# Row pairs of a query projection in two groups a step, with other places for four kinds of copies

## The chip, the cores and the metric

The kernel runs on one NeuronCore of a Trainium2 chip. The metric is the device time of one execution in microseconds (us), as a median over runs. Beside these runs there is one profiled execution, from which the profile page and the trace come; its own time is given with its span, which is the time from its first to its last instruction.

## The reference

Two kinds of layer, A and B, each used twice with the same weights, on x of 2048 tokens with 448 features:

```
x = x + A(layernorm(x));  x = x + B(layernorm(x))
x = x + A(layernorm(x));  x = x + B(layernorm(x))

A: mem = mem0 (8 rows)
   for each segment s of 32 tokens (64 segments):
       h = concat(mem, x[s])                  # 40 rows
       q, k, v = h Wq, h Wk, h Wv             # 16 heads of 256
       o = softmax(mask(q k^T / 16)) v Wo     # masked: mem rows see all, others are causal
       mem = o[:8];  out[s] = o[8:]
B: h = relu(x W_gate) * (x W_up);  out = h W_down      # 1792 hidden
```

The memory rows of a segment come out of the segment before, so layer A is a recurrence of 64 steps, run twice.

## The kernel before

Before the loop the kernel folds Wq and Wk of each head into one 448 x 448 matrix (`A_sb`, `A3`, `A3z`) and Wv and Wo into another (`B_sb`). The main loop runs over steps `g` from 0 to 68 (`step`, L610). In a step the first layer A works on segment g (chain 0) and the second layer A on segment g - 4 (chain 1), side by side in the columns of the same matmuls. Steps 0 to 3 and 64 to 67 have one chain, steps 4 to 63 have two. Every second step also carries layer B for blocks of tokens (`Feed`, L419): here it is called a feed step, the others plain steps.

The query projection of a step multiplies 448 features. 384 of them are done in wide matmuls of 128 rows, three for each of 56 tiles of weights (`close_bank`, L532). The last 64 features need only 64 rows, so two such matmuls with different row halves of TensorE run as a row pair (`open_banks`, L519). Ten PSUM banks are filled: for half 0 of the heads banks 0 to 3 (six tiles each, called b0 to b3 in the code) and a tail bank z0 (four tiles); for half 1 c0 to c3 and z1. Before the change a bank is opened by its row pairs and closed by its wide matmuls. The order at the start of a step is: pairs of b0, b2; close both; pairs of b1, b3, z0, z1; close z0, b1, b3, z1; transposes of the layer's input (`kps`, in `hk_make`) and pairs of c0 to c3; scores of half 0's memory queries (`scores_m(0)`, tile `Sm`); close c0, c2, c1, c3. Closing ends with a copy of the bank to SBUF: banks 0 to 3 to `TQ` by the engine named in the call, a tail bank to `TZ` in two halves, one by VectorE and one by ScalarE.

Then follow a transposition of the weights of the memory queries (`flipped`: PE `pps`, then a VectorE copy to `PT`, L589), the scores `Sx` of half 0, the weighting by PT (`weigh_m`, tiles `ya` and `yb`), in feed steps the transposes `tps` of `Feed.xposed`, then `scores_m(1)` (the second `Sm`) and `Sx` of half 1, and the output projection into the bank `ox`, with gate, up and down matmuls of layer B between its parts in a feed step. At the end `finish` (L747) copies ox to the next step's memory columns (`hT`, L211, VectorE) and to `OT` (L752, ScalarE), and `weigh_x(1, ...)` makes the columns `Y` or `Z` for the next step. In a feed step `Feed.residual` (L430) transposes `OT` (tiles `otp`) behind the closing of b2 and adds it to the rows `xa` on VectorE.

PSUM has one bank with the tag `ox` and seven with the tag `ps`. The ox bank also takes one half of each `flipped_dims` (L162), kps and otp. The order on TensorE is written out by hand: `mm` and `tr` (L81, L84) tie every instruction to the one before. On the other engines a scheduler sets the order, except where `tc.keep_in_program_order` pins an instruction; it also picks which of the seven banks a tile gets.

Of the kernel before, what the change touches and what calls it, by code (L numbers as in the profile page):

```python
# [20 lines left out]
SEG = 32  # L21
# [32 lines left out]
def build_kernel(ctx, tc, A_x, A_mem0, A_Wq, A_Wk, A_Wv, A_Wo, B_W_gate, B_W_up, B_W_down, out,  # L54
# [26 lines left out]
    def mm(*a, **k):  # L81
        in_order(nc.tensor.matmul(*a, **k))  # L82

    def tr(*a):  # L84
        in_order(nc.tensor.transpose(*a))  # L85
# [5 lines left out]

    def evac(eng, dst, src):
        if eng is nc.scalar:
            nc.scalar.copy(dst, src)  # L94
        else:
            eng.tensor_copy(dst, src)  # L96


    xa = [glob.tile([P, DM], BF, name=f"xa{i}") for i in range(3)]
# [59 lines left out]
        t = glob.tile([P, 5, 6, 64], BF, name=f"TQ{hf}")  # L159
        TQ.append(t)  # L160

    def flipped_dims(name, src):  # L162

        two = [psum.tile([P, 4, 64], BF, name=name, **where) for where in (dict(tag="ox", bufs=1), dict(tag="ps"))]
        for kd in range(4):
            for r in range(2):
                tr(two[r][:, kd, :], src(r, kd), ident[ROWS[r], ROWS[r]])
        return two

    def row_stats(t, pin=False):  # L170

# [247 lines left out]
    class Feed:  # L419


        def __init__(self, i):
# [4 lines left out]
            self.x = xa[i % 3]  # L427
            self.nx = xp[i % 2]

        def residual(self):  # L430
            tp = flipped_dims("otp", lambda r, kd: OT[ROWS[r], kd, :])
            xd = self.x[:].rearrange("p (c d) -> p c d", d=64)
            for r in range(2):
                nc.vector.tensor_tensor(xd[:, r::2, :], tp[r][:, 0:4 - r, :], xd[:, r::2, :], op=ALU.add)
            self.st = row_stats(self.x)
# [63 lines left out]
    class Bank:  # L499


        def __init__(self, hf, i):
            self.hf = hf
            self.i = i
            self.tiles = [tidx(kd, i // 2, 2 * (i % 2) + k) for kd in range(3) for k in range(2)] if i < 4 else                 list(range(24, NT))
            self.ps = psum.tile([P, 512], F32, tag="ps", name="prj")

        def out(self, t, n):
            k = self.tiles.index(t)
# [6 lines left out]
        kd, eo, p4 = t // 8, t // 4 % 2, t % 4  # L516
        return eo, A3[ROWS[eo], hf, 4 * kd + p4, :]

    def open_banks(chains, hb, j, *which):  # L519

        n = L * len(chains)
        banks = [Bank(hf, i) for hf, i in which]
        for a, b in zip(banks[::2], banks[1::2]):
            for k in range(len(a.tiles)):
                for bk in (a, b):
                    t = bk.tiles[k]
                    r, w = last_rows(bk.hf, t)
                    mm(bk.out(t, n), w, moving(hb, j, 3, chains, ROWS[r]), start=(k == 0), stop=False,
                       skip_group_check=True)
        return banks  # L530

    def close_bank(bk, chains, hb, j, eng):  # L532

        n = L * len(chains)
        hf, N = bk.hf, len(bk.tiles)
        for t in bk.tiles:
            for kd in range(3):
                mm(bk.out(t, n), A_sb[:, kd, hf, t, :], moving(hb, j, kd, chains), start=False, stop=(kd == 2),
                   skip_group_check=True)
        ps = bk.ps  # L540
        if bk.i < 4:
            at = 2 * (bk.i // 2) + bk.i % 2
            parts = [(eng, slice(0, P), TQ[hf][:].rearrange("p g (k b) w -> p g k (b w)", b=2)[:, :, :, 32 * at:32 * at + 32], 3)]
        else:
            parts = [(nc.vector, slice(0, 64), TZ[hf][0:64, :, 0:64].unsqueeze(2), 1),
                     (nc.scalar, slice(64, 128), TZ[hf][0:64, :, 64:128].unsqueeze(2), 1)]
        for eng, rows, T, K in parts:
            T = T.rearrange("p g k (t q) -> p k t g q", q=16)
            if len(chains) == 2:
                evac(eng, T, ps[rows, 0:N * n].rearrange("p (k t g q) -> p k t g q", k=K, t=N // K, q=16))  # L550
                continue
            c = chains[0]
            src = ps[rows, 0:N * n].rearrange("p (k t w) -> p k t w", k=K, t=N // K)
            x, m = (0, SEG) if c == 0 else (MEM, 0)
            evac(eng, T[:, :, :, 2, MEM * c:MEM * c + MEM], src[:, :, :, m:m + MEM])
            evac(eng, T[:, :, :, 3 * c:3 * c + 2, :],
                 src[:, :, :, x:x + SEG].rearrange("p k t (g q) -> p k t g q", q=16))

    def queries(hf, g, kd):
        return TQ[hf][:, g, 2 * kd:2 * kd + 2, :] if kd < 3 else TZ[hf][:, g, :]  # L560
# [49 lines left out]
    def step(g, ff):  # L610
# [9 lines left out]
        def ys(hf, later=0):  # L620
            return YY[hf][(g + later) % 2]

        def hk_make():
            kps = flipped_dims("kps", lambda r, kd: hb[ROWS[r], j, kd * HI:kd * HI + HI])
            hk = HK[g % 2]
            for r, eng in enumerate((nc.vector, nc.scalar)):
                evac(eng, hk[:, 0:4, 64 * r:64 * r + 64], kps[r][:])
            nc.scalar.copy(hk[:].rearrange("p k n -> p (k n)")[:, 512:768].rearrange("p (a b) -> p a b", b=64)[:, 0::3, :],
                           kps[1][:, 3, :].unsqueeze(1).to_broadcast([P, 2, 64]))
            return hk  # L630
# [53 lines left out]
        def weigh_x(hf, hk, PT):  # L684

            def keep(eng, c, t0, src):
                n = src.shape[-1] // SEG
                dst = ys(hf, 1)[:, t0:t0 + n, XO[c]:XO[c] + SEG]
                k = max(1, n // 8)
                evac(eng, dst.rearrange("p (k i) (e q) -> p k e i q", k=k, q=16),  # L690
                     src.rearrange("p (k e i q) -> p k e i q", k=k, e=2, q=16))

            y1 = {c: psum.tile([P, 512], F32, tag="ps", name=f"y1_{c}") for c in chains}
            for kd in range(2):
# [48 lines left out]
        def ot_cols(c):  # L743
            o = (g - 1) % BLK * SEG + (TB if c == 0 else 0)
            return OT[:, :, o:o + SEG]

        def finish():  # L747
            if ms:
                src = ox[:, :, M0:M0 + 16].rearrange("p k (c m) -> p k c m", m=MEM)
                set_mem(g + 1, src[:, :, ms[0]:ms[-1] + 1, :], ms, 3)  # L750
            for c in xs:
                nc.scalar.copy(ot_cols(c)[:, 0:3], ox[:, :, XO[c]:XO[c] + SEG])  # L752

        def feed(*us):
            if ff is not None:
# [16 lines left out]

        load_some()
        nc.gpsimd.tensor_copy(hb[ROWS[0], j, 4 * HI:4 * HI + 104], hb[ROWS[0], j, 3 * HI:3 * HI + 104])
        b0, b2 = open_banks(chains, hb, j, (0, 0), (0, 2))
        close_bank(b0, chains, hb, j, nc.vector)
        close_bank(b2, chains, hb, j, nc.scalar)
        if ff is not None:
            ff.residual()
            ff.norm(nc.gpsimd)  # L780
        b1, b3, z0, z1 = open_banks(chains, hb, j, (0, 1), (0, 3), (0, 4), (1, 4))
        close_bank(z0, chains, hb, j, None)
        load_some()
        close_bank(b1, chains, hb, j, nc.vector)
        close_bank(b3, chains, hb, j, nc.scalar)
        close_bank(z1, chains, hb, j, None)
        hk = hk_make()
        c0, c2, c1, c3 = open_banks(chains, hb, j, (1, 0), (1, 2), (1, 1), (1, 3))
        scores_m(0)
        close_bank(c0, chains, hb, j, nc.scalar)  # L790
        close_bank(c2, chains, hb, j, nc.scalar)
        close_bank(c1, chains, hb, j, nc.vector)
        close_bank(c3, chains, hb, j, nc.scalar)
        if len(chains) == 2:
            pm = flipped(PM[0], 1, "m0")
            Sx0 = scores_x(0)
            weigh_m(0, hk, pm)
            if ff is not None:
# [62 lines left out]
        step(g, Feed(i) if g % 2 and 0 <= i < nblk + LAG // BLK - 1 else None)  # L861

    ff = Feed(nblk + LAG // BLK - 1)
    ff.residual()
    ff.norm()
    ff.xposed()
# [62 lines left out]
```

## Time and profile before

| | |
|---|---|
| median of 3 runs | 1579.52 us (1578.43 to 1586.14) |
| profiled execution | 1585.95 us, its span 1584.0 us |
| mean granted TensorE clock | 0.990 |
| TensorE matmuls busy | 1552.8 us, 98% of the span |
| VectorE busy | 1112.6 us, 70% |
| ScalarE busy | 783.1 us, 49% |
| GpSimd busy | 174.9 us, 11% |

Matmuls overlap in a pipeline, so the busy time of TensorE is the time in which at least one is under way, and the mean length of one (some 0.2 us for 80 columns) is far over the time from one start to the next. What a matmul costs is read from start times.

### The profile page before, as it was taken

Reading aid. Unit: us, or ns where it says so; the run is one execution under the profiler, and the core shown is the slowest. Engines: PE = TensorE matmul, PEld = TensorE weight load, DVE = VectorE, ACT = ScalarE, POOL = GpSimd, SP = SyncE. Lnnn points to the kernel's source line nnn. Section 1 sums busy time; section 2 is a strip of 40 time slices with the busy share of each in tenths; the row PEclk is TensorE's granted clock in tenths of the full one; section 3 lists DMA queues with packets and bytes.
Section 4 is the critical chain, followed back from the end, with each engine's and each line's share of the span. In section 5 each row is a group of like instructions: output and inputs, shape, how many; then the busy total and the mean of one; then the engine's idle time right before and its main releaser. Section 6 shows DMA issues by size and latency. Waiting matters only on the chain.

```text
span 1584.0 us, 98180 instructions
## 1 busy us (share of the span) xinstructions
PE 1552.8 (98%) x45116; PEld 1426.0 (90%) x45116; DVE 1112.6 (70%) x3825; ACT 783.1 (49%) x2307; POOL 174.9 (11%) x308
## 2 busy tenths in 40 slices
PE   9889999999999999999999999999999999999997
PEld 7588899999999999999999999999999999999885
DVE  6755677776777777776777677777767777777663
ACT  6634445544455545554455545544445545544442
POOL 3201110111011111111011111011001111011110
PEclk9989999999999999999999999999999999999998
DMA  9530000000000000000000000000000000000000
GB/s 284 148 80 8 9 10 5 9 10 10 10 10 10 10 10 6 8 10 10 10 10 10 10 10 7 7 10 10 10 10 10 10 10 8 6 8 7 7 7 6
DMA packets 29469, 33.13 MB, mean 21 GB/s; under 512 B 3320, under 2 KB 28160, under 8 KB 29056
## 3 DMA queue, kind: packets, MB, share of 16 engines
q1 hardware_dynamic: 28848, 26.74, 6.2%
q8 instruction: 353, 5.78, 1.5%
q14 instruction: 60, 0.49, 0.1%
q10 hardware_dynamic: 144, 0.11, 0.1%
q0 software_dynamic: 64, 0.01, 0.0%
HBM read 23.18 MB, written 1.84 MB: 16 GB/s over the span
## 4 chain that ended last, share of the span: by engine, by line
PE 95%; DVE 2%; issue 1%; ACT 1%; DMA 1%; POOL 1%; SPq 0%; POOLq 0%; ACTq 0%; DVEq 0%
PE prj L82 30%; PE ox L82 25%; PE ups L82 10%; PE dps L82 6%; PE o L82 5%; PE y L82 4%; PE Sx L82 3%; PE Sm L82 2%; PE aps L82 1%; PE pps L85 1%; PE gps L82 1%; PE bps L82 1%; PE tps L85 1%; PE kps L85 1%; PE ym L82 1%
## 5 line engine op out<-in xcount | busy, mean ns | idle before, releaser
L82 PEld LDWEIGHTS <-B_sb 128*128 128x128 bf16 (+1 forms) x15456 | 495.1, 103 | 29.6 <-issue 21.6
L82 PE MATMUL prj<-hT,A_sb 128*128 128x80 bf16 (+1 forms) x11424 | 430.7, 200 | 0.1
L82 PEld LDWEIGHTS <-A_sb 128*128 128x128 bf16 x11424 | 406.3, 100 | 8.5 <-issue 0.2
L82 PE MATMUL ox<-Y,B_sb 128*128 128x80 bf16 (+4 forms) x5880 | 223.1, 199 | 1.9 <-DVE Y L661 1.9
L94 ACT CAST TQ<-prj 128x480 bf16<-128x480 f32 (+1 forms) x380 | 183.1, 494 | 83.7 <-PE prj L82 59.2
L82 PE MATMUL ox<-Z,B_sb 128*128 128x80 bf16 (+2 forms) x5712 | 217.6, 199 | 1.3 <-DVE Z L661 1.3
L82 PE MATMUL ups<-xT,Wgu_sb 64*128 64x128 bf16 (+1 forms) x3332 | 191.3, 214 | 1.3 <-DVE hh L458 0.8
L82 PE MATMUL gps<-xT,Wgu_sb 64*128 64x128 bf16 (+1 forms) x3332 | 191.3, 214 | 0.4 <-ACT xT L444 0.3
L82 PEld LDWEIGHTS <-Wgu_sb 64*128 64x128 bf16 x6664 | 179.7, 95 | 4.4 <-issue 2.3
L96 DVE CAST TQ<-prj 128x480 bf16<-128x480 f32 (+1 forms) x228 | 129.5, 574 | 17.3 <-PE prj L82 11.7
L458 DVE SCALAR_TENSOR_TENSOR hh<-gps,ut 128x256 bf16<-128x256 f32 (+1 forms) x238 | 94.5, 407 | 48.2 <-ACT ut L457 35.4
L457 ACT CAST ut<-ups 128x256 bf16<-128x256 f32 (+1 forms) x238 | 85.5, 359 | 82.7 <-PE gps L82 64.1
L94 ACT CAST Y<-y 64x128 bf16<-64x128 f32 (+2 forms) x256 | 89.4, 379 | 46.5 <-DVE Y L96 41.5
L96 DVE CAST Y<-y 64x128 bf16<-64x128 f32 (+2 forms) x256 | 102.2, 420 | 14.2 <-ACT Y L94 4.3
L94 ACT COPY hT<-tps 128x256 bf16<-128x256 bf16 x32 | 11.9, 372 | 199.0 <-DVE hT L96 199.0
L96 DVE CAST Z<-y 64x128 bf16<-64x128 f32 (+2 forms) x256 | 99.2, 418 | 12.4 <-ACT Z L94 5.5
L589 DVE COPY PT<-pps 128x128 bf16<-128x128 bf16 (+1 forms) x206 | 49.9, 256 | 80.5 <-PE pps L85 77.7
L94 ACT CAST Z<-y 64x128 bf16<-64x128 f32 (+2 forms) x256 | 89.2, 378 | 23.8 <-DVE Z L96 17.4
L82 PE MATMUL dps<-Wd_sb,hh 128*128 128x448 bf16 x476 | 99.3, 362 | 0.0
L94 ACT CAST TZ<-prj 64x320 bf16<-64x320 f32 (+2 forms) x152 | 56.1, 380 | 86.4 <-DVE TZ L96 78.5
L577 DVE TENSOR_REDUCE ssum<-se 128x2 f32<-128x80 f32 (+1 forms) x270 | 70.8, 274 | 35.8 <-ACT se L571 33.6
L82 PE MATMUL prj<-hT,A 64*128 64x80 bf16 (+1 forms) x3264 | 93.9, 196 | 1.8 <-issue 1.4
(130 smaller groups left out, 2265.7 us busy)
## 6 DMA issues: line engine op xcount, KB each, us to landing
wo<-in_A_Wo_dram SPq DMA_DIRECT2D x8, 448.0 KB, 5.1
nat<-in_A_Wq_dram SPq DMA_DIRECT2D x8, 384.0 KB, 6.1
nat<-in_A_Wk_dram SPq DMA_DIRECT2D x8, 384.0 KB, 6.2
nat<-in_A_Wv_dram SPq DMA_DIRECT2D x8, 384.0 KB, 6.1
xa<-in_A_x_dram SPq DMA_DIRECT2D x32, 56.0 KB, 2.3
xa<-xp SPq DMA_DIRECT2D x32, 56.0 KB, 1.9
out_dram<-xa SPq DMA_DIRECT2D x32, 56.0 KB, 2.0
xp<-in_A_x_dram SPq DMA_DIRECT2D x30, 56.0 KB, 2.1
```

The costliest lines, as they stand in the source:

```text
L82: in_order(nc.tensor.matmul(*a, **k))
L85: in_order(nc.tensor.transpose(*a))
L94: nc.scalar.copy(dst, src)
L96: eng.tensor_copy(dst, src)
L457: nc.scalar.copy(ut[:, :, n], ups[:, :, n])
L458: nc.vector.scalar_tensor_tensor(out=hh[:, 2 * u:2 * u + 2, n], in0=gps[:, :, n], scalar=0.0, in1=ut[:, :, n], op0=ALU.max, op1=ALU.mult)
L577: nc.vector.tensor_reduce(ssum[:], se[:], axis=AX.X, op=ALU.add)
L589: nc.vector.tensor_copy(PT[:], pps[:].rearrange("p b q -> p (b q)"))
```

## The change

- `open_banks` and `close_bank` are taken apart. `pairs` issues row pairs for banks that may be empty or may already hold their wide matmuls; `wide` issues wide matmuls, all or some tiles; `leave_bank` copies a bank out.
- The step now has two groups of row pairs. The first holds b0 and b2, the transposes of the layer's input (`flipped_dims`, now tiles `flip0` in the ox bank and `flip1`), and in a feed step the OT transposes (`flip_out`), right behind those pairs and in the same two banks. The second stands behind the wide matmuls of b0, b2, b1, z0 and holds the pairs of z0, z1, b1, b3, c0, c2, c1, c3. It closes z0 and b1.
- c0 is placed in the ox bank. `scores_m(0)` comes after b3, z1 and four of c0's six tiles.
- Both halves of a tail bank are copied by one engine, ScalarE. b3 moves from ScalarE to VectorE.
- With two chains, c1's copy (VectorE) is placed behind `flipped(PM[0])` and pinned; c0's copy (ScalarE) is pinned.
- The copies from ox to OT move from ScalarE to VectorE, behind the copy to hT, and the VectorE copy of the first Y tile of `weigh_x(1, ...)` is pinned behind them.
- `hk_make` reads the transposes made at the start of the step. Its copies and the residual now come earlier.

The number of matmuls, transposes and elements copied is unchanged. In the order of the built program, VectorE's list in a step with two chains reads: PM's weights, PT, c1's copy, Y from ya, the two maxima.

The diff, with what the text speaks of:

```diff
@@ -159,13 +158,17 @@
         t = glob.tile([P, 5, 6, 64], BF, name=f"TQ{hf}")
         TQ.append(t)
-    def flipped_dims(name, src):
-
-        two = [psum.tile([P, 4, 64], BF, name=name, **where) for where in (dict(tag="ox", bufs=1), dict(tag="ps"))]
+    def flip_banks():
+
+        return [psum.tile([P, 8, 64], BF, name=f"flip{r}", **where)
+                for r, where in enumerate((dict(tag="ox", bufs=1), dict(tag="ps")))]
+
+    def flipped_dims(two, at, src):
+
         for kd in range(4):
             for r in range(2):
-                tr(two[r][:, kd, :], src(r, kd), ident[ROWS[r], ROWS[r]])
-        return two
+                tr(two[r][:, at + kd, :], src(r, kd), ident[ROWS[r], ROWS[r]])
+        return [t[:, at:at + 4, :] for t in two]
     def row_stats(t, pin=False):
@@ -427,8 +430,11 @@
             self.x = xa[i % 3]
             self.nx = xp[i % 2]
+        def flip_out(self, two):
+            self.tp = flipped_dims(two, 4, lambda r, kd: OT[ROWS[r], kd, :])
+
         def residual(self):
-            tp = flipped_dims("otp", lambda r, kd: OT[ROWS[r], kd, :])
+            tp = self.tp
             xd = self.x[:].rearrange("p (c d) -> p c d", d=64)
             for r in range(2):
                 nc.vector.tensor_tensor(xd[:, r::2, :], tp[r][:, 0:4 - r, :], xd[:, r::2, :], op=ALU.add)
@@ -499,11 +505,12 @@
     class Bank:
-        def __init__(self, hf, i):
+        def __init__(self, hf, i, **where):
             self.hf = hf
+            self.empty = True
             self.i = i
             self.tiles = [tidx(kd, i // 2, 2 * (i % 2) + k) for kd in range(3) for k in range(2)] if i < 4 else                 list(range(24, NT))
-            self.ps = psum.tile([P, 512], F32, tag="ps", name="prj")
+            self.ps = psum.tile([P, 512], F32, name="prj", **(where or dict(tag="ps")))
         def out(self, t, n):
             k = self.tiles.index(t)
@@ -516,38 +523,46 @@
         kd, eo, p4 = t // 8, t // 4 % 2, t % 4
         return eo, A3[ROWS[eo], hf, 4 * kd + p4, :]
-    def open_banks(chains, hb, j, *which):
+    def pairs(banks, chains, hb, j):
         n = L * len(chains)
-        banks = [Bank(hf, i) for hf, i in which]
         for a, b in zip(banks[::2], banks[1::2]):
             for k in range(len(a.tiles)):
                 for bk in (a, b):
                     t = bk.tiles[k]
                     r, w = last_rows(bk.hf, t)
-                    mm(bk.out(t, n), w, moving(hb, j, 3, chains, ROWS[r]), start=(k == 0), stop=False,
+                    mm(bk.out(t, n), w, moving(hb, j, 3, chains, ROWS[r]), start=(bk.empty and k == 0), stop=not bk.empty,
                        skip_group_check=True)
-        return banks
-
-    def close_bank(bk, chains, hb, j, eng):
+                    if t == bk.tiles[-1]:
+                        bk.empty = False
+
+    def wide(bk, chains, hb, j, tiles=slice(0, 6)):
+
+        n = L * len(chains)
+        for t in bk.tiles[tiles]:
+            for kd in range(3):
+                mm(bk.out(t, n), A_sb[:, kd, bk.hf, t, :], moving(hb, j, kd, chains),
+                   start=(bk.empty and kd == 0 and t == bk.tiles[0]), stop=(not bk.empty and kd == 2),
+                   skip_group_check=True)
+        bk.empty = False
+
+    def leave_bank(bk, chains, eng, pin=False):
         n = L * len(chains)
         hf, N = bk.hf, len(bk.tiles)
-        for t in bk.tiles:
-            for kd in range(3):
-                mm(bk.out(t, n), A_sb[:, kd, hf, t, :], moving(hb, j, kd, chains), start=False, stop=(kd == 2),
-                   skip_group_check=True)
         ps = bk.ps
         if bk.i < 4:
             at = 2 * (bk.i // 2) + bk.i % 2
             parts = [(eng, slice(0, P), TQ[hf][:].rearrange("p g (k b) w -> p g k (b w)", b=2)[:, :, :, 32 * at:32 * at + 32], 3)]
         else:
-            parts = [(nc.vector, slice(0, 64), TZ[hf][0:64, :, 0:64].unsqueeze(2), 1),
-                     (nc.scalar, slice(64, 128), TZ[hf][0:64, :, 64:128].unsqueeze(2), 1)]
+            parts = [(eng, slice(0, 64), TZ[hf][0:64, :, 0:64].unsqueeze(2), 1),
+                     (eng, slice(64, 128), TZ[hf][0:64, :, 64:128].unsqueeze(2), 1)]
         for eng, rows, T, K in parts:
             T = T.rearrange("p g k (t q) -> p k t g q", q=16)
             if len(chains) == 2:
-                evac(eng, T, ps[rows, 0:N * n].rearrange("p (k t g q) -> p k t g q", k=K, t=N // K, q=16))
+                r = evac(eng, T, ps[rows, 0:N * n].rearrange("p (k t g q) -> p k t g q", k=K, t=N // K, q=16))
+                if pin:
+                    tc.keep_in_program_order(r)
                 continue
             c = chains[0]
             src = ps[rows, 0:N * n].rearrange("p (k t w) -> p k t w", k=K, t=N // K)
@@ -555,6 +570,11 @@
             evac(eng, T[:, :, :, 2, MEM * c:MEM * c + MEM], src[:, :, :, m:m + MEM])
             evac(eng, T[:, :, :, 3 * c:3 * c + 2, :],
                  src[:, :, :, x:x + SEG].rearrange("p k t (g q) -> p k t g q", q=16))
+
+    def close_bank(bk, chains, hb, j, eng):
+
+        wide(bk, chains, hb, j)
+        leave_bank(bk, chains, eng)
     def queries(hf, g, kd):
         return TQ[hf][:, g, 2 * kd:2 * kd + 2, :] if kd < 3 else TZ[hf][:, g, :]
@@ -620,11 +640,10 @@
         def ys(hf, later=0):
             return YY[hf][(g + later) % 2]
-        def hk_make():
-            kps = flipped_dims("kps", lambda r, kd: hb[ROWS[r], j, kd * HI:kd * HI + HI])
+        def hk_make(kps):
             hk = HK[g % 2]
             for r, eng in enumerate((nc.vector, nc.scalar)):
-                evac(eng, hk[:, 0:4, 64 * r:64 * r + 64], kps[r][:])
+                evac(eng, hk[:, 0:4, 64 * r:64 * r + 64], kps[r])
             nc.scalar.copy(hk[:].rearrange("p k n -> p (k n)")[:, 512:768].rearrange("p (a b) -> p a b", b=64)[:, 0::3, :],
                            kps[1][:, 3, :].unsqueeze(1).to_broadcast([P, 2, 64]))
             return hk
@@ -687,8 +706,10 @@
                 n = src.shape[-1] // SEG
                 dst = ys(hf, 1)[:, t0:t0 + n, XO[c]:XO[c] + SEG]
                 k = max(1, n // 8)
-                evac(eng, dst.rearrange("p (k i) (e q) -> p k e i q", k=k, q=16),
-                     src.rearrange("p (k e i q) -> p k e i q", k=k, e=2, q=16))
+                r = evac(eng, dst.rearrange("p (k i) (e q) -> p k e i q", k=k, q=16),
+                         src.rearrange("p (k e i q) -> p k e i q", k=k, e=2, q=16))
+                if eng is nc.vector and hf == 1 and t0 == 0:
+                    tc.keep_in_program_order(r)
             y1 = {c: psum.tile([P, 512], F32, tag="ps", name=f"y1_{c}") for c in chains}
             for kd in range(2):
@@ -749,7 +770,7 @@
                 src = ox[:, :, M0:M0 + 16].rearrange("p k (c m) -> p k c m", m=MEM)
                 set_mem(g + 1, src[:, :, ms[0]:ms[-1] + 1, :], ms, 3)
             for c in xs:
-                nc.scalar.copy(ot_cols(c)[:, 0:3], ox[:, :, XO[c]:XO[c] + SEG])
+                nc.vector.tensor_copy(ot_cols(c)[:, 0:3], ox[:, :, XO[c]:XO[c] + SEG])
         def feed(*us):
             if ff is not None:
@@ -772,27 +793,43 @@
         load_some()
         nc.gpsimd.tensor_copy(hb[ROWS[0], j, 4 * HI:4 * HI + 104], hb[ROWS[0], j, 3 * HI:3 * HI + 104])
-        b0, b2 = open_banks(chains, hb, j, (0, 0), (0, 2))
+        b0, b2 = Bank(0, 0), Bank(0, 2)
+        pairs((b0, b2), chains, hb, j)
+        two = flip_banks()
+        kps = flipped_dims(two, 0, lambda r, kd: hb[ROWS[r], j, kd * HI:kd * HI + HI])
+        if ff is not None:
+            ff.flip_out(two)
         close_bank(b0, chains, hb, j, nc.vector)
         close_bank(b2, chains, hb, j, nc.scalar)
         if ff is not None:
             ff.residual()
             ff.norm(nc.gpsimd)
-        b1, b3, z0, z1 = open_banks(chains, hb, j, (0, 1), (0, 3), (0, 4), (1, 4))
-        close_bank(z0, chains, hb, j, None)
+        hk = hk_make(kps)
         load_some()
-        close_bank(b1, chains, hb, j, nc.vector)
-        close_bank(b3, chains, hb, j, nc.scalar)
-        close_bank(z1, chains, hb, j, None)
-        hk = hk_make()
-        c0, c2, c1, c3 = open_banks(chains, hb, j, (1, 0), (1, 2), (1, 1), (1, 3))
+        b1, z0 = Bank(0, 1), Bank(0, 4)
+        wide(b1, chains, hb, j)
+        wide(z0, chains, hb, j)
+        b3, z1 = Bank(0, 3), Bank(1, 4)
+        c0 = Bank(1, 0, tag="ox", bufs=1)
+        c2, c1, c3 = (Bank(1, i) for i in (2, 1, 3))
+        pairs((z0, z1, b1, b3), chains, hb, j)
+        leave_bank(z0, chains, nc.scalar)
+        leave_bank(b1, chains, nc.vector)
+        pairs((c0, c2, c1, c3), chains, hb, j)
+        close_bank(b3, chains, hb, j, nc.vector)
+        close_bank(z1, chains, hb, j, nc.scalar)
+        wide(c0, chains, hb, j, slice(0, 4))
         scores_m(0)
-        close_bank(c0, chains, hb, j, nc.scalar)
+        wide(c0, chains, hb, j, slice(4, 6))
+        leave_bank(c0, chains, nc.scalar, True)
         close_bank(c2, chains, hb, j, nc.scalar)
-        close_bank(c1, chains, hb, j, nc.vector)
+        wide(c1, chains, hb, j)
+        if len(chains) == 1:
+            leave_bank(c1, chains, nc.vector)
         close_bank(c3, chains, hb, j, nc.scalar)
         if len(chains) == 2:
             pm = flipped(PM[0], 1, "m0")
+            leave_bank(c1, chains, nc.vector, True)
             Sx0 = scores_x(0)
             weigh_m(0, hk, pm)
             if ff is not None:
@@ -861,6 +898,7 @@
         step(g, Feed(i) if g % 2 and 0 <= i < nblk + LAG // BLK - 1 else None)
     ff = Feed(nblk + LAG // BLK - 1)
+    ff.flip_out(flip_banks())
     ff.residual()
     ff.norm()
     ff.xposed()
```

More of the change, by code (lines that the diff above doesn't have):

```diff
@@ L93, in evac @@
         if eng is nc.scalar:
-            nc.scalar.copy(dst, src)
-        else:
-            eng.tensor_copy(dst, src)
+            return nc.scalar.copy(dst, src)
+        return eng.tensor_copy(dst, src)
     xa = [glob.tile([P, DM], BF, name=f"xa{i}") for i in range(3)]
```

## The prediction

> **What bounds the kernel now.** I read the page first: its busy times and the chain that ended last.
>
> ```profile
> PE 1552.8 (98%) x45116; PEld 1426.0 (90%) x45116; DVE 1112.6 (70%) x3825; ACT 783.1 (49%) x2307; POOL 174.9 (11%) x308
> PE 95%; DVE 2%; issue 1%; ACT 1%; DMA 1%; POOL 1%; SPq 0%; POOLq 0%; ACTq 0%; DVEq 0%
> ```
>
> TensorE is busy throughout and carries 95% of the chain. So a copy on another engine costs nothing unless TensorE waits for it, and a TensorE gap costs its whole length: none is given back. Next I read the timeline of one step that works on two chains and has no feed-forward (a plain step). A line is start, time from there to the end of the merged row, engine, source line, operation.
>
> ```profile
> 813.95 0.21 DVE L211 CAST hT<-ox 128x48 bf16<-128x48 f32 x1
> 814.32 0.39 PE L82 MATMUL prj<-hT,A 64*128 64x80 bf16 x12
> 814.64 1.46 PE L82 MATMUL prj<-hT,A_sb 128*128 128x80 bf16 x36
> 816.04 0.39 PE L82 MATMUL prj<-hT,A 64*128 64x80 bf16 x12
> 816.26 0.31 PE L82 MATMUL prj<-hT,A3z 64*128 64x80 bf16 x8
> 816.50 2.32 PE L82 MATMUL prj<-hT,A_sb 128*128 128x80 bf16 x60
> ...
> 818.76 0.29 PE L85 MATMUL kps<-ident,hT 64*128 64x64 bf16 x8
> 818.88 0.59 PE L82 MATMUL prj<-hT,A 64*128 64x80 bf16 x24
> 819.41 0.28 PE L82 MATMUL Sm<-hT,TQ 128*128 128x80 bf16 x3
> ...
> 821.70 0.66 DVE L96 CAST TQ<-prj 128x480 bf16<-128x480 f32 x1 [0.17 <-PE prj L82]
> 822.14 0.22 PE L85 MATMUL pps<-ident,PM 128*128 128x128 bf16 x1
> 822.35 0.56 ACT L94 CAST TQ<-prj 128x480 bf16<-128x480 f32 x1 [0.73 <-PE prj L82]
> 822.40 0.23 DVE L589 COPY PT<-pps 128x128 bf16<-128x128 bf16 x1
> 822.68 0.27 PE L82 MATMUL ya<-PT,hk 128*128 128x128 bf16 x2
> 822.80 0.33 DVE L568 TENSOR_REDUCE mx<-Sx 128x4 f32<-128x160 f32 x1 [0.17 <-PE Sx L82]
> 822.96 0.28 PE L82 MATMUL Sm<-hT,TQ 128*128 128x80 bf16 x3
> 823.04 0.41 DVE L661 CAST Y<-ya 128x256 bf16<-128x256 f32 x1
> ```
>
> Three things are to be seen. The matmuls of 64 rows (pairs and kps) stand in three visits, at 814.32, 816.04 and 818.76. Wide matmuls stand between them: 36 take 814.64 to 816.04 (1.40 us), 60 take 816.50 to 818.76 (2.26), so one takes 0.86/24 = 0.036 us, and 1.40 - 36 x 0.036 leaves 0.11 us for changing back to 64 rows. And the second Sm, at 822.96, stands right behind ScalarE's copy of c3 (822.35 + 0.56 = 822.91), 0.05 us after its end, as ya stands 0.05 after PT's (822.63).
>
> The same place in a step with feed-forward (a feed step) has four transposes (tps) before that Sm:
>
> ```profile
> 840.20 0.22 PE L85 MATMUL pps<-ident,PM 128*128 128x128 bf16 x1
> 840.96 0.39 PE L85 MATMUL tps<-ident,xn 128*128 128x128 bf16 x4
> 841.18 0.27 PE L82 MATMUL Sm<-hT,TQ 128*128 128x80 bf16 x3
> ```
>
> **The change part by part.** Steps 4 to 63 have two chains, 30 plain and 30 feed.
>
> *Three visits become two: a gain.* No matmul is added or dropped. A visit of 12 pairs takes 814.64 - 814.32 = 0.32 us, one of 20 takes 0.46, one of 32 takes 0.65. At 0.018 us a pair (24 pairs from 818.88 to Sm, 0.53 less 0.10 of change) the first leaves 0.10 for changing to 128 rows. A visit less saves 0.11 + 0.10 = 0.21 us, in feed steps too, where the OT flips already sit inside a visit. Bounds 0.19 to 0.23.
>
> *Copies out of ox on VectorE: a small wait.* The flips now come right behind the first 12 pairs, into the bank of ox. In a plain step that is 814.32 + 12 x 0.018 = 814.54. The bank must be read out first: hT<-ox ends 814.16, then two OT copies. VectorE shows no 128x96 copy; 128x48 takes 0.208 us, 64x128 takes 0.286, ScalarE's 128x96 takes 0.242. I take 0.25, between the two VectorE rows. Independent copies overlap by 0.08 (mx from 822.80 would end 823.13, the next starts 823.04). So: 814.08 to 814.33, 814.25 to 814.50, plus 0.05 is 814.55: wait 0.01. In a feed step (hT<-ox ends 832.14, pairs start 832.27) the flips wait from 832.48 to 832.53, 0.05. Bounds 0 and, with 0.286, 0.12.
>
> *c3's bank in a feed step: a small wait.* In the built program c3 takes the bank of b2, which ScalarE empties. VectorE, from 832.48, has y1 (0.69, overlapped), two y2 pieces that follow ScalarE's read of that bank (to 833.8), y2 (0.42) and the two residual adds (0.45 by the row of L434): 834.6. ScalarE's copies of flip1 (0.375 and 0.265) come behind the adds, since the program lets two engines read one bank only in turn, to 835.35; b2's copy (0.555) ends 835.93, so c3 may start at 835.98. TensorE would be there at 832.53 + 16 flips 0.23 + change 0.10 + 66 wide 2.37 + change 0.10 + 32 pairs 0.57 = 835.90. Wait 0.08, bounds 0 and 0.2. In a plain step no residual is ahead and 0.3 us is spare.
>
> *Half 0's scores: a small wait.* Sm0 needs b3's copy, now on VectorE and only two part-banks earlier. From b3's first wide matmul: the last starts at 17 x 0.036 = 0.61, VectorE 0.25 later (b1 before: last matmul 817.54, copy 817.79), 0.657 us of copy, 0.05 to resume: 1.57. TensorE arrives after 18 + 12 + 12 wide: 1.51. Wait 0.06, bounds 0 and 0.1.
>
> *c1's copy behind PT: the large wait.* Before, VectorE copied c1 at 821.70, ahead of PT. In the built program its list reads PT, then c1's copy, then Y<-ya. PT needs pps, and pps stands behind all of c3. From pps: PT starts +0.26, takes 0.224; the copy starts 0.08 before its end, +0.40, takes 0.657 (mean of that form 0.655), ends +1.06; Sm1 restarts at +1.11. Before, Sm1 stood at +0.82 in plain steps (822.96 - 822.14) and +0.98 in feed steps. Wait added: 0.29 and 0.13. Queued behind it on VectorE are Y<-ya, the maxima and, in feed steps, xT; each still ends before its reader (ox starts 0.56 after Sm1, Y<-ya ends 0.28 after it; PX is needed 3.1 after it and ends at 2.8; xT on ScalarE ends 2.8 us after pps, and the gate matmuls reach those rows at 3.2).
>
> *Softmax of PM: nothing, but thin.* Sm0 to PM's end takes 2.11 (819.41 to 821.52). TensorE now has 60 wide matmuls instead of 72 behind Sm0: 0.15 + 2.15 = 2.30 until pps. Cover left 0.13 plain, 0.07 feed; without it, each step pays the difference.
>
> *TZ on one engine, OT off ScalarE:* ScalarE is 49% busy and its TZ copies end before exp is due (1.50 against 1.77 us after z1's start): nothing. Bank choice, waits and code around it: nothing found on the path.
>
> *One-chain steps (8):* 0.21 saved each, but two-piece copies make Sm0 wait about 0.1 to 0.2; the waits view from 69 to 149 us has 1.8 us on prj, part of which is start-up. I take 0 in all, bounds -4 and +3.
>
> Sum: plain -0.21 + 0.01 + 0.06 + 0.29 = +0.15; feed -0.21 + 0.05 + 0.08 + 0.06 + 0.13 = +0.11; 30 x 0.26 = +7.8. The profiled execution took 1585.95 us (span 1584.0), so 1593.8; it stood 6.4 above the median 1579.52, so the median becomes 1587.3. About 0.5% (7.9 us) is what a measurement here can tell from no change.
>
> **The rivals.** *The small waits are covered* (not slower). The terms of 0.01 to 0.08 sit on durations known to a few hundredths. If the OT copies, b2's and b3's copies finish just ahead of TensorE, there remain 30 x (-0.42 + 0.42) = 0: 1579.5. The turning point is 0.06 us a step. For it: each wait is a small difference of long sums. Against: all err towards waiting, as c1's does not cancel. Chance 0.35, with part-cover up to 1584.
>
> *The edges win* (faster). The early one-chain steps lose their prj waits wholly, -6 us, and the small waits are covered too: 1573.5, and 1571 where the switches save 0.23 (68 x 0.02 = 1.4) and the last steps 1 us more. Part of the wait there is "issue", not a bank. Chance 0.06.
>
> *PM comes too late* (slower still). If ScalarE's four TZ copies or VectorE push PM 0.2 us later, its cover is gone and pps waits about 0.1: +6, 1593.3. The rows put exp 0.27 after the copies. Chance 0.12.
>
> *No overlap on VectorE.* If c1's copy starts only at PT's end, Sm1 waits 0.084 more, 60 x 0.084 = 5 us: 1592.3. The rows at 822.80 and 823.04 show overlap. Chance 0.05. The Trainium skill's page "VectorE: DVE Perf Modes", section "The DRAIN you can't avoid", says that the next operation does not start until the pipe is empty. By that rule this rival holds; the two rows named here do not agree with it for independent operations.
>
> **How the numbers follow.** The forecast of 1587.3 has 0.42, the rest as named. It sits at the edge of what can be told (1587.4): in its own range, 1583 to 1592, about 0.28 of the 0.42 is beyond it, since a wait that I missed can only add. With the two slower rivals (0.17) slower by over 0.5% is 0.45; faster 0.06; within 0.5% is 0.49 (0.35 covered and 0.14 of the forecast's own). Range 1577 to 1596: from a little below the covered case to PM late.
>
> **What would show it.** Right: two visits a step at 64 rows; Sm1 1.1 us after pps in both kinds of step; Sm0 just behind b3's copy. Wrong: Sm1 at 0.8 after pps, PM waited for at pps, or plain steps shorter than 17.95 us (814.32 to 832.27) by more than 0.05.

## The result, and the profile after

The changed kernel takes 1602.09 us (median of 4 runs, 1600.97 to 1604.59) against 1582.83 us for the kernel before, in the same comparison (4 runs, 1578.43 to 1586.84): ratio 1.0127, 95% interval 1.0102 to 1.0152. It is slower by about 19 us. The forecast was +7.8 us and 1587.3 us, with a range from 1577 to 1596.

The profiled execution took 1600.97 us (span 1599.2), 15.0 more than that of before, at the same granted clock of 0.99. The page of the changed kernel, first the busy times and then the chain that ended last:

```profile
PE 1555.1 (97%) x45116; PEld 1428.2 (89%) x45116; DVE 1102.9 (69%) x3877; ACT 778.0 (49%) x2255; POOL 175.5 (11%) x308
PE 84%; DVE 9%; ACT 3%; issue 2%; DMA 1%; POOL 1%; SPq 0%; POOLq 0%; DVEq 0%; ACTq 0%
```

TensorE is as busy as before to within 2.3 us, but the span grew by 15.2: the time is new waiting. The chain shows for whom. VectorE's share of it went from 2% to 9%, while VectorE's own busy time fell by 9.7 us. So it is not the amount of work on VectorE that hurts but its place.

The timeline of one plain step of the changed kernel (start, time to the end of the row, engine, line, operation):

```profile
820.83 0.39 PE L82 MATMUL prj<-hT,A 64*128 64x80 bf16 x12
821.05 0.29 PE L85 MATMUL flip<-ident,hT 64*128 64x64 bf16 x8
821.28 2.54 PE L82 MATMUL prj<-hT,A_sb 128*128 128x80 bf16 x66
823.75 0.32 PE L82 MATMUL prj<-hT,A3z 64*128 64x80 bf16 x8
823.90 0.81 PE L82 MATMUL prj<-hT,A 64*128 64x80 bf16 x36
824.64 1.68 PE L82 MATMUL prj<-hT,A_sb 128*128 128x80 bf16 x42
826.21 0.28 PE L82 MATMUL Sm<-hT,TQ 128*128 128x80 bf16 x3
...
828.51 0.22 PE L85 MATMUL pps<-ident,PM 128*128 128x128 bf16 x1
...
828.72 0.56 ACT L94 CAST TQ<-prj 128x480 bf16<-128x480 f32 x1 [0.28 <-PE prj L82]
828.77 0.23 DVE L609 COPY PT<-pps 128x128 bf16<-128x128 bf16 x1 [0.44 <-PE pps L85]
...
828.91 0.65 DVE L95 CAST TQ<-prj 128x480 bf16<-128x480 f32 x1
...
829.06 0.29 PE L82 MATMUL ya<-PT,hk 128*128 128x128 bf16 x2
...
829.71 0.27 PE L82 MATMUL Sm<-hT,TQ 128*128 128x80 bf16 x3 [0.25 <-DVE TQ L95]
```

Two visits of 64-row matmuls are left (820.83 and 823.75). ScalarE's copy of c3 ends at 829.28, where the second Sm could have followed it. But it stands at 829.71, behind c1's copy on VectorE (828.91 + 0.65 = 829.56), and the row names that copy as its releaser. VectorE had been idle for 0.44 us ahead of PT: c1's bank was full and nobody copied it, since the copy is placed and pinned behind PT.

The feed step of the changed kernel carries a second new wait, some 4 us further on. In these rows `mx`, `se`, `ssum`, `rs` and `PX` are the maxima, subtraction and exp, sums, reciprocals and weights of the softmax; `ppr` are the transposes of these weights; `ups` and `gps` are matmuls of a gate and up unit of layer B:

```profile
848.05 0.27 PE L82 MATMUL Sm<-hT,TQ 128*128 128x80 bf16 x3
...
849.24 0.32 DVE L588 TENSOR_REDUCE mx<-Sx 128x4 f32<-128x160 f32 x1
849.60 0.50 ACT L591 ACTIVATE se<-se 128x80 f32<-128x80 f32 x2
...
850.36 0.15 DVE L599 RECIPROCAL rs<-ssum 128x2 f32<-128x2 f32 x1
...
850.44 0.30 DVE L590 TENSOR_TENSOR se<-Sx,mx 128x160 f32<-128x160 f32 x1
...
850.83 0.34 ACT L591 ACTIVATE se<-se 128x160 f32<-128x160 f32 x1 [0.74 <-DVE rs L601]
...
851.79 0.32 DVE L602 TENSOR_TENSOR PX<-se,rs 128x160 bf16<-128x160 f32 x1
...
852.04 0.75 DVE L464 SCALAR_TENSOR_TENSOR hh<-gps,ut 128x256 bf16<-128x256 f32 x2
...
852.15 0.22 PE L85 MATMUL ppr<-ident,PX 64*128 64x64 bf16 x4
852.51 0.21 PE L82 MATMUL ups<-xT,Wgu_sb 64*128 64x128 bf16 x1
```

`hh` is the product of gate and up on VectorE; it frees the bank of the first gate unit. The fourth gate and up unit starts at 852.51, 0.05 us after the end of the first of the two hh (852.04, each 0.42 long), and the waits view below names hh as its releaser, so its bank is the one that hh frees. It starts 0.33 us after the last start of `ppr`, where 0.03 is usual. The same stretch of VectorE and ScalarE in the kernel before:

```profile
842.28 0.31 DVE L568 TENSOR_REDUCE mx<-Sx 128x4 f32<-128x160 f32 x1
842.63 0.32 DVE L570 TENSOR_TENSOR se<-Sx,mx 128x160 f32<-128x160 f32 x1
842.87 0.72 ACT L571 ACTIVATE se<-se 128x80 f32<-128x80 f32 x3
...
844.27 0.55 DVE L582 TENSOR_TENSOR PX<-se,rs 128x160 bf16<-128x160 f32 x2
844.74 0.76 DVE L458 SCALAR_TENSOR_TENSOR hh<-gps,ut 128x256 bf16<-128x256 f32 x2
```

Before, the third subtraction `se` (from the second Sx) ran right behind its maxima and all three exp ran in one row. In the changed kernel it stands in VectorE's list behind the sums and a reciprocal of the first two. So its exp comes late, and PX and hh with it: hh starts 3.99 us after the second Sm instead of 3.56.

The waits view of the changed kernel (engine, line, what was waited for: total, times, longest) names both, for 300 to 1480 us of the span. It attributes only part of the occurrences; the start times show both in every such step:

```profile
PE Sm L82 <- DVE TQ L95: 6.6, 26, 0.3
PE ups L82 <- DVE hh L464: 1.6, 4, 0.4
```

Nearly all step lengths of a kind agree within some 0.01 us in a trace, so they tell more than medians of whole runs. A step is measured from the start of its first row pairs to that of the next step; the table has the median over the steps of a kind. "Sm1 after pps" is the second Sm's start after that of pps, plain / feed; the unit's gap is the 0.33 above.

| kernel | time, us | ratio to before (interval) | plain | feed | Sm1 after pps | unit's gap |
|---|---|---|---|---|---|---|
| before | 1580.5 to 1582.8 in four comparisons | 1 | 17.95 | 26.51 | 0.82 / 0.98 | 0.03 |
| after | 1602.09 | 1.0127 (1.0102 to 1.0152) | 18.19 | 26.93 | 1.19 / 1.19 | 0.33 |
| before_c1_behind | 1607.12 | 1.0175 (1.0161 to 1.0189) | 18.33 | 27.03 | 1.19 / 1.19 | 0.32 |
| c1_scalar | 1576.12 | 0.9966 (0.9951 to 0.9982) | 17.89 | 26.43 | 0.90 / 1.00 | 0.03 |
| c1_ahead | 1573.28 | 0.9955 (0.9940 to 0.9970) | 17.81 | 26.52 | 0.82 / 1.09 | 0.03 |
| c1_last_scalar | 1595.24 | 1.0099 (1.0084 to 1.0114) | 18.27 | 26.77 | 1.28 / 1.33 | 0.03 |
| se_ahead | 1590.66 | 1.0060 (1.0037 to 1.0083) | 18.19 | 26.62 | 1.19 / 1.19 | 0.03 |
| three_visits | 1609.86 | 1.0186 (1.0162 to 1.0209) | 18.34 | 27.07 | 1.19 / 1.19 | 0.33 |
| ot_scalar | 1603.84 | 1.0143 (1.0123 to 1.0164) | 18.27 | 27.01 | 1.19 / 1.19 | 0.32 |
| mix | 1570.87 | 0.9942 (0.9929 to 0.9954) | 17.81 | 26.43 | 0.82 / 1.00 | 0.03 |
| mix_5 | 1573.71 | 0.9962 (0.9949 to 0.9976) | 17.84 | 26.44 | 0.91 / 1.03 | 0.03 |

For the changed kernel the steps give 30 x (0.245 + 0.42) = +20.0 us, which is the measured +19. Five feed steps take 0.2 to 0.27 us more than the others. In four of them ScalarE starts the third exp 0.28 us later although its input is ready as early as elsewhere, and hh and the unit follow; why it starts late is open. In the two profiled executions the difference is 15.0 and not 20: the parts of the trace outside the two-chain steps are 5 us shorter. Most of that is one step with one chain, the fourth, which took 25.8 us in the profile of before and 22.3 in that of after: before has a gap of 1.6 us there that is put down to issue, and down matmuls that start 0.37 us apart where 0.19 is usual.

### The profile page after: what moved, and what is told of

It reads as the page before. It is cut to its first block, busy times and chain, and to the rows that moved or that the text cites. A ratio compares the mean times of both kernels' runs of the same rounds, so it can differ in the third digit from the quotient of the medians.

```text
span 1599.2 us, 98218 instructions
## 1 busy us (share of the span) xinstructions
PE 1555.1 (97%) x45116; PEld 1428.2 (89%) x45116; DVE 1102.9 (69%) x3877; ACT 778.0 (49%) x2255; POOL 175.5 (11%) x308
## 4 chain that ended last, share of the span: by engine, by line
PE 84%; DVE 9%; ACT 3%; issue 2%; DMA 1%; POOL 1%; SPq 0%; POOLq 0%; DVEq 0%; ACTq 0%
PE prj L82 29%; PE ox L82 23%; PE dps L82 6%; PE ups L82 5%; PE o L82 5%; PE y L82 4%; PE gps L82 3%; DVE TQ L95 2%; ACT xT L450 2%; PE Sm L82 1%; DVE ssum L597 1%; PE aps L82 1%; PE pps L85 1%; PE bps L82 1%; PE Sx L82 1%
## 5 line engine op out<-in xcount | busy, mean ns | idle before, releaser
L82 PEld LDWEIGHTS <-B_sb 128*128 128x128 bf16 (+1 forms) x15456 | 495.1, 103 | 27.7 <-issue 19.8
L95 DVE CAST TQ<-prj 128x480 bf16<-128x480 f32 (+2 forms) x304 | 171.2, 570 | 65.7 <-PE prj L82 65.6
L94 ACT CAST TQ<-prj 128x480 bf16<-128x480 f32 (+2 forms) x304 | 142.2, 500 | 25.7 <-PE prj L82 15.0
L94 ACT CAST TZ<-prj 64x320 bf16<-64x320 f32 (+2 forms) x304 | 112.1, 379 | 79.1 <-PE prj L82 75.5
L591 ACT ACTIVATE se<-se 128x80 f32<-128x80 f32 (+1 forms) x270 | 76.9, 301 | 99.5 <-DVE se L590 75.4
L597 DVE TENSOR_REDUCE ssum<-se 128x2 f32<-128x80 f32 (+1 forms) x270 | 74.0, 275 | 37.9 <-ACT se L591 36.7
L82 PEld LDWEIGHTS <-TQ 128*128 128x128 bf16 x1938 | 80.3, 96 | 17.8 <-ACT TQ L94 10.7
```

Of the source, the lines that this page charges most:

```text
L94: return nc.scalar.copy(dst, src)
L95: return eng.tensor_copy(dst, src)
L591: nc.scalar.activation(se[:], se[:], AF.Exp, scale=SCALE)
L597: nc.vector.tensor_reduce(ssum[:], se[:], axis=AX.X, op=ALU.add)
```

## The experiments

The theory before them: the visits saved are real, and the loss is c1's copy behind PT, directly (the second Sm) and, in feed steps, through a late hh. The main rival: VectorE is late because it also received b3's copy and the copies out of ox.

**One part alone, on the kernel before** (before_c1_behind; `close_bank` is split into `wide` and `leave_bank` for it, which is not shown):

```diff
-        close_bank(c1, chains, hb, j, nc.vector)
+        wide(c1, chains, hb, j)
+        if len(chains) == 1:
+            leave_bank(c1, chains, nc.vector)
         close_bank(c3, chains, hb, j, nc.scalar)
         if len(chains) == 2:
             pm = flipped(PM[0], 1, "m0")
+            leave_bank(c1, chains, nc.vector, True)
```

> The kernel before, with one part of the change alone: c1's copy is placed behind pps and PT on VectorE. Theory: the second Sm moves from 0.82 us (plain) and 0.98 us (feed) after pps to 1.19 in both, and in feed steps the fourth gate and up unit waits 0.3 us: plain step 17.95 + 0.38 = 18.33, feed step 26.51 + 0.21 + 0.30 = 27.02, over 30 of each 27 us more than the kernel before. Rival (it takes VectorE's other new copies too): the second Sm at 1.1 and no wait at the unit, plain 18.2, feed 26.65, 12 us more.

Its timeline in a plain step:

```profile
831.23 0.22 PE L85 MATMUL pps<-ident,PM 128*128 128x128 bf16 x1
...
831.49 0.23 DVE L600 COPY PT<-pps 128x128 bf16<-128x128 bf16 x1 [0.88 <-PE pps L85]
831.63 0.65 DVE L95 CAST TQ<-prj 128x480 bf16<-128x480 f32 x1
...
832.42 0.27 PE L82 MATMUL Sm<-hT,TQ 128*128 128x80 bf16 x3 [0.27 <-DVE TQ L95]
```

Plain 18.33 and feed 27.03, as the theory said to 0.01: 30 x (0.385 + 0.518) = 27.1 us, and the ratio of 1.0175 says 27.7. VectorE's order in the feed step that follows is again that of the changed kernel: the third subtraction (853.24) stands behind the sums and a reciprocal (853.17). No other part of the change is in this kernel, so placing and pinning this one copy makes both waits, and the rival is out.

**The copy elsewhere** (c1_scalar: by ScalarE, right behind c1's matmuls; c1_ahead: by VectorE at the same place, so ahead of PT). The edits on the changed kernel, each with one of the two added lines:

```diff
         wide(c1, chains, hb, j)
-        if len(chains) == 1:
-            leave_bank(c1, chains, nc.vector)
+        leave_bank(c1, chains, nc.scalar if len(chains) == 2 else nc.vector)   # c1_scalar
+        leave_bank(c1, chains, nc.vector)                                      # c1_ahead
         close_bank(c3, chains, hb, j, nc.scalar)
...
-            leave_bank(c1, chains, nc.vector, True)
```

> Theory (the loss is c1's copy behind PT on VectorE, and in feed steps the hh that is late behind it): with ScalarE making c1's copy right after c1's matmuls, the second Sm stands 0.9 us after pps in plain steps and 1.0 in feed steps instead of 1.19, the wait of the fourth gate and up unit falls from 0.33 us to under 0.1, a plain step takes 17.9 us instead of 18.19 and a feed step 26.4 instead of 26.93: some 25 us less than the changed kernel, 1576 to 1580. Rival (VectorE is late because it now also has b3's copy and the copies out of ox): the second Sm moves but the unit's wait stays at 0.3, feed step 26.7. Rival (two visits save nothing): plain step 18.0 or more.

> c1's copy stays on VectorE, but right behind c1's matmuls, ahead of PT. Theory: PT is some 0.17 us later and ya with it, the second Sm stands 0.9 to 1.0 us after pps in plain steps and 1.15 in feed steps, Y from ya and the maxima no longer stand behind the copy, so the unit's wait in feed steps is mostly gone: plain step 17.95 to 18.0, feed step 26.55 to 26.65, some 15 to 20 us less than the changed kernel. Rival (overloaded VectorE): unit's wait stays at 0.3, feed step 26.9.

Both lose the two waits and end under the kernel before. c1_scalar came as expected in every number. c1_ahead was better than expected, most of all in plain steps (17.81 against 17.95 to 18.0): VectorE began c1's copy early enough that PT was hardly delayed, and the second Sm again follows c3's copy at 0.82. In its feed steps PT does start later, since the copy is still running when pps is done:

```profile
831.54 0.24 DVE L602 TENSOR_TENSOR PM<-se,rs 128x80 bf16<-128x80 f32 x1
831.70 0.65 DVE L95 CAST TQ<-prj 128x480 bf16<-128x480 f32 x1
831.91 0.22 PE L85 MATMUL pps<-ident,PM 128*128 128x128 bf16 x1
...
832.27 0.22 DVE L609 COPY PT<-pps 128x128 bf16<-128x128 bf16 x1
832.54 0.28 PE L82 MATMUL ya<-PT,hk 128*128 128x128 bf16 x2
```

ya stands 0.63 after pps instead of 0.54, and those 0.09 us are what c1_ahead loses to c1_scalar in a feed step (26.52 against 26.43).

**Late, but not on VectorE** (c1_last_scalar, an edit of the changed kernel):

```diff
-            leave_bank(c1, chains, nc.vector, True)
+            leave_bank(c1, chains, nc.scalar, True)
```

> c1's copy still comes behind pps, but on ScalarE behind c3's copy, so nothing on VectorE stands behind it. The second Sm is then late (some 1.35 us after pps, as c3's copy ends 0.77 after it and c1's takes 0.5), but Y from ya and the maxima are not. Theory that the unit's wait comes from VectorE's row behind c1's copy: the wait of 0.3 is gone, plain step 18.19 + 0.15 = 18.35, feed step 26.93 + 0.15 - 0.30 = 26.8. Rival (the unit waits because the second Sm itself is late): the wait stays, feed step 27.1. For the restart: if 0.14 us belongs to a wait on VectorE and ScalarE together, the second Sm starts 0.05 after the copy's end here, else 0.14.

A feed step, with c3's and c1's copies in one row on ScalarE:

```profile
843.20 0.22 PE L85 MATMUL pps<-ident,PM 128*128 128x128 bf16 x1
843.46 1.02 ACT L94 CAST TQ<-prj 128x480 bf16<-128x480 f32 x2 [0.28 <-PE pps L85]
...
844.53 0.28 PE L82 MATMUL Sm<-hT,TQ 128*128 128x80 bf16 x3 [0.17 <-ACT TQ L94]
...
847.74 0.41 DVE L464 SCALAR_TENSOR_TENSOR hh<-gps,ut 128x256 bf16<-128x256 f32 x1
```

The second Sm is later than in the changed kernel (1.33 after pps), and yet hh starts 3.21 us after it and the unit waits for nothing. So a late second Sm does not make hh late; something on VectorE does. (The plain step came to 18.27 instead of 18.35, since c1's copy overlaps c3's on ScalarE by 0.1 us and ends 0.46 after it.) And the Sm starts 0.05 us after the copy's end (843.46 + 1.02 = 844.48), not 0.15.

**Only the order behind it** (se_ahead): c1's copy stays behind PT; in feed steps the third subtraction is pinned ahead of the sums (the parameters that carry the pins and the branch for plain steps are not shown).

```diff
...
+            if ff is not None:
+                three = [scores_m(1, True)]
+                Sx1 = scores_x(1)
+                three.append(weights_begin(Sx0, 4, PX[0], None, "x0"))
+                half1 = weights_begin(Sx1, 4, PX[1], None, "x1", True)
+                weights_end(*three[0], pin=True)
+                weights_end(*three[1])
...
```

> The changed kernel, with c1's copy left behind PT; only in feed steps, VectorE's third subtraction for exp (se from the second Sx) is put back ahead of the sums, as it stood before the change. In the changed kernel it starts 0.91 us after its maxima end, behind the wait for exp, the sums and a reciprocal. If this order is what makes hh late, the second Sm stays at 1.19 us after pps and plain steps at 18.19, hh starts some 3.55 us after the second Sm instead of 3.99, the unit's wait of 0.3 is gone and a feed step takes 26.63: 30 x 0.30 = 9 us less than the changed kernel, 1593. If what makes hh late is c1's copy and the maxima in the row ahead, whatever the order behind, the wait stays near 0.3 and so does the time.

A feed step of it:

```profile
840.88 0.27 PE L82 MATMUL Sm<-hT,TQ 128*128 128x80 bf16 x3
...
842.07 0.31 DVE L588 TENSOR_REDUCE mx<-Sx 128x4 f32<-128x160 f32 x1
842.42 0.32 DVE L590 TENSOR_TENSOR se<-Sx,mx 128x160 f32<-128x160 f32 x1
842.43 0.74 ACT L593 ACTIVATE se<-se 128x80 f32<-128x80 f32 x3
...
844.30 0.90 DVE L464 SCALAR_TENSOR_TENSOR hh<-gps,ut 128x256 bf16<-128x256 f32 x2
```

hh starts 3.42 after the second Sm (expected 3.55), the unit's wait is gone, a feed step takes 26.62 (expected 26.63), and the plain step is unmoved. The steps give 30 x 0.32 = 9.5 us less than the changed kernel; the medians, from two comparisons, differ by 11.4. This corrects the theory: hh was late not because c1's copy and the maxima were queued ahead of it, but because the scheduler, with that copy placed and pinned there, put one subtraction behind three operations that wait for exp. Whether the place or the pin made it do so was not tested: no run has the copy behind PT without the pin. The 0.30 us belong to the order, the other 0.21 and 0.38 to the copy itself.

**The price of a visit, and of the copies out of ox** (three_visits, ot_scalar), both on the changed kernel:

```diff
-        pairs((c0, c2, c1, c3), chains, hb, j)                 # three_visits
         close_bank(b3, chains, hb, j, nc.vector)
+        pairs((c0, c2, c1, c3), chains, hb, j)                 # three_visits
...
-                nc.vector.tensor_copy(ot_cols(c)[:, 0:3], ox[:, :, XO[c]:XO[c] + SEG])   # ot_scalar
+                nc.scalar.copy(ot_cols(c)[:, 0:3], ox[:, :, XO[c]:XO[c] + SEG])          # ot_scalar
```

> The pairs of c0 to c3 stand behind b3 and z1's side again, as a third visit of 64-row matmuls after b3's. Theory: a visit costs 0.21 us, and b3's copy gets 0.06 more time, which takes the first Sm's wait away: plus 0.15 us in each of the 60 steps, plain step 18.34, feed step 27.08, some 9 us more than the changed kernel. Rival (changing between 64 and 128 rows costs nothing): no change or 0.06 us less a step.

> The copies from ox to OT go back to ScalarE. Theory (c1's copy is the cause): the second Sm stays at 1.19 us after pps, the unit's wait at 0.3; the flips wait some 0.05 us more in each step: same or up to 4 us more than the changed kernel. Rival (VectorE overloaded): the second Sm and the unit's wait come earlier by part of the 0.4 us taken off VectorE, feed steps 0.1 to 0.3 us shorter, 3 to 9 us less.

A plain step of three_visits:

```profile
826.44 0.38 PE L82 MATMUL prj<-hT,A 64*128 64x80 bf16 x12
826.76 0.82 PE L82 MATMUL prj<-hT,A_sb 128*128 128x80 bf16 x18
827.51 0.60 PE L82 MATMUL prj<-hT,A 64*128 64x80 bf16 x24
828.04 1.03 PE L82 MATMUL prj<-hT,A_sb 128*128 128x80 bf16 x24
828.91 0.27 PE L82 MATMUL Sm<-hT,TQ 128*128 128x80 bf16 x3
```

A step is longer by 0.147 (plain) and 0.143 (feed), where 0.15 was worked out: a visit costs 0.20 to 0.21, and of that the first Sm's wait of 0.058 is paid back. Here the first Sm follows the wide matmul ahead of it by 0.036, as one wide matmul follows another, where the changed kernel shows 0.094.

In ot_scalar the two copies of OT on ScalarE end later, and the flips wait for them:

```profile
821.40 0.38 ACT L773 CAST OT<-ox 128x96 bf16<-128x96 f32 x2
...
821.84 0.29 PE L85 MATMUL flip<-ident,hT 64*128 64x64 bf16 x8
```

Each step is 0.08 longer (expected 0.05 to 0.07), and neither the second Sm nor the unit's gap moves. So with the flips at this place, moving these copies to VectorE was worth 0.08 us a step; it is a part of the change that pays. The medians of whole runs (1603.84 and 1602.09) are too close to show it.

**A version faster than both kernels** (mix), and one step further (mix_5), on the changed kernel:

```diff
         wide(c1, chains, hb, j)
-        if len(chains) == 1:
-            leave_bank(c1, chains, nc.vector)
+        leave_bank(c1, chains, nc.scalar if ff is not None and len(chains) == 2 else nc.vector)
...
-            leave_bank(c1, chains, nc.vector, True)
...
-        wide(c0, chains, hb, j, slice(0, 4))                   # mix_5
+        wide(c0, chains, hb, j, slice(0, 5))                   # mix_5
         scores_m(0)
-        wide(c0, chains, hb, j, slice(4, 6))                   # mix_5
+        wide(c0, chains, hb, j, slice(5, 6))                   # mix_5
```

> c1's copy right behind its matmuls, on VectorE in plain steps and on ScalarE in feed steps, each the shorter step of the two kernels that had one place for both: plain 17.81, feed 26.43, so 30 x 0.09 = 2.7 us less than with VectorE in both, 1570 to 1572. If the copies of one step delay the next, the two do not add up and it stays at 1573.

> The same, and half 0's first scores after five of c0's tiles instead of four. The wait of 0.058 us ahead of the first Sm is covered (three more wide matmuls, 0.108), but PM has only 0.07 us to spare in plain steps and 0.13 in feed steps, and comes 0.05 later against a pps that is 0.06 earlier. So plain 0.02 less, feed 0.06 less: some 2 us less, 1568 to 1570. If PM is the bound in both, no gain.

mix takes 1570.87 us, ratio 0.9942 (0.9929 to 0.9954): the better step of each kind adds up. In its page the chain that ended last is TensorE's again:

```profile
PE 95%; DVE 2%; ACT 1%; issue 1%; DMA 1%; POOL 1%; SPq 0%; POOLq 0%; ACTq 0%; DVEq 0%
```

mix_5 gains nothing (plain 17.84, feed 26.44). The first Sm moves back 0.05 us, and what follows it has no room. In feed steps pps now starts 0.057 after PM's end, which is the usual restart, so PM has become the bound. In plain steps everything on VectorE is 0.1 later against pps: c1's copy, and behind it PT, so ya stands 0.68 after pps instead of 0.57. The expectation had the spare times the wrong way round (0.13 us is the plain step's, 0.07 the feed step's) and did not see PT behind the copy.

## Why the prediction was wrong

The direction and the place of the loss were right; its size was under half. Term by term, in us a step:

| step of the prediction | predicted, plain / feed | measured, plain / feed |
|---|---|---|
| a visit less | -0.21 / -0.21 | -0.21 / -0.20 |
| flips behind the copies out of ox | 0.01 / 0.05 | 0 / 0.04 |
| c3's bank | none / 0.08 | none / none |
| first Sm behind b3's copy | 0.06 / 0.06 | 0.058 / 0.058 |
| second Sm behind c1's copy | 0.29 / 0.13 | 0.38 / 0.21 |
| readers behind c1's copy ("each still ends before its reader") | 0 / 0 | 0 / 0.30 |
| sum | 0.15 / 0.11 | 0.23 / 0.41 |
| step length | | 0.245 / 0.42 |

**The step that failed** is the sentence on what is queued behind c1's copy on VectorE. It went through Y from ya, the maxima, xT and the first PX, whose 3.1 us until it is needed are those of a plain step (822.96 to 826.04 in before), found each in time, and stopped there. In the feed step, a few operations on, the order of VectorE's list had changed, and the reader that suffered was hh, 4 us later, through the chain se, exp, sum, reciprocal, PX, hh. That order stood in the built program and could have been read. It cost 30 x 0.30 = 9 us, and with it the forecast would have been 1596, the upper end of the range.

**The mis-sized term** is the restart of the second Sm. The prediction took the 0.05 us of the rows it had shown. The trace of after has 0.147 between the end of c1's copy and the Sm, in every two-chain step: +1.19 after pps instead of the +1.11 predicted. Over 60 steps that is about 5 us more. With the 9 us of the order that makes 14 us; c3's bank, below, gives 2.4 back, and the forecast fell short by some 12. The start of that copy was right: it overlaps PT by 0.09 (828.91 against 828.77 + 0.23). So the rival "no overlap on VectorE" fell, although its price of 5 us is about what the restart took. The section "The DRAIN you can't avoid" of the Trainium skill's page "VectorE: DVE Perf Modes" was weighed only by its first sentences; it goes on to say that a next operation that is not held starts earlier, and this trace agrees with that.

**Too high** was c3's bank in feed steps. From the step's first pairs, b2's copy was to end at +3.66 and ended at +3.52 (839.03 to 842.55). ScalarE's copies in a row overlap by some 0.1 us (hk ends 842.08, b2's copy starts 841.97), which was counted for VectorE but not for ScalarE. In the feed step's sum this 0.08 and the 0.08 that the restart lacked cancel, which is luck. About 0.01 to 0.02 us of each step's growth is in no row of the table and stays open.

**Right** were the price of a visit (three_visits), the first Sm's wait, PM just in time (after's spare time at pps is 0.13 plain and 0.07 feed, as worked out), and that VectorE's load itself would not be the bound (ot_scalar). "The small waits are covered" held for c3's bank and the flips of the plain step, and not for the first Sm; "the edges win" did not happen. The parts outside the two-chain steps were put at 0; what the medians leave for them is within 2 us of that, while in the two profiled executions they differ by 5.

## What to carry to other kernels

Placing and pinning one instruction in an engine's list can let a scheduler rearrange what follows it, as it did here. Compare the two lists until they agree again, and follow every operation that changed places through the other engines to the matmul that reads it, also where that lies some microseconds off. And a copy whose bank is full should not be put behind something that waits for TensorE while its engine stands idle: here VectorE idled 0.44 us ahead of PT and then held up TensorE by 0.38. When a regrouping and a reordering come in one change, time them apart; here a visit less gained 0.21 us a step, and one reordered copy lost about twice that.

## What the runs showed of the hardware

The time from the end of a copy to the matmul that waits for it was not one number. It was 0.055 us where the weight load waited for one engine only (c1_last_scalar, where all four c banks are ScalarE's), and 0.147 where Sm needed a last copy on VectorE besides those on ScalarE (after, before_c1_behind: 0.146). In after, the wait for VectorE is then a separate instruction on TensorE ahead of the weight load (829.60 to 829.65 in the plain step shown), and the weight load, at 829.68, itself waits for ScalarE. That this extra instruction is what costs the 0.09 us fits both cases. It also fits ya and, in after, the first Sm, whose weight loads wait for VectorE alone: ya starts 0.057 us after PT's end, the first Sm 0.05 after b3's copy (825.50 + 0.66, then 826.21). It was not tested by itself. The section "Identifying Dependency Chains" of the Trainium skill's page "Perfetto Trace Analysis" says that an instruction that waits for several engines may have such instructions put in front of it; it gives no price for it.
